# One load of k for three of four batches, pooled by GpSimd from its form with zeros

## The chip, the cores and the metric

The kernel runs on one core of a Trainium2 chip, as one program. The metric is its time on the device in microseconds (us), lower is better. A core has TensorE (matrix products, with a granted clock of 1.2 or 2.4 GHz), VectorE, ScalarE and GpSimd, each with a queue of instructions of its own that is worked off in order, and SyncE, which here issues the loads. In the profile's rows they are PE (PEld for its weight loads), DVE, ACT, POOL and SP.

## What is computed

An attention at two resolutions, then two expert layers. The change is in the attention, for 4 batches, 8 heads, 576 positions and 64 columns per head:

```python
q_d = q.reshape(B, H, Sd, factor, D).mean(axis=3)      # factor 4, Sd = 144; k_d, v_d alike
out_d = sm_attn(q_d, k_d, v_d)
out_up = np.repeat(out_d, factor, axis=2)
mask = np.abs(pos[:, None] - pos[None, :]) < factor
scores = np.where(mask, scale * np.matmul(q, k.transpose(0, 1, 3, 2)), -1000000000.0)
# softmax over the last axis, then
return (out_up + np.matmul(attn, v)).astype(np.float32)
```

So q, k and v are each needed twice: whole, for a local attention of 7 positions, and pooled over 4 neighbours, for the coarse one. Behind it the 2304 tokens are routed to 8 experts, and all go through a second layer.

## The kernel before

**Units.** Attention is a list of 60 units, made by `units`: a local unit `("l", b, i)` takes block `i` of 10 of batch `b`, all heads at once, and a pooled unit `("c", b, p)` takes head pair `p` of 4 (`p = 4` the rest of all pairs). The five pooled units of batch 0 come first; those of batch `b + 1` stand between the local units of batch `b`, behind its blocks 3, 5, 6, 8 and 9. Unit positions count through the list, so c1,0 (pooled, batch 1, pair 0) is four positions behind l0,0, c1,1 seven, c1,2 nine. `run` works it as a pipeline: scores (TensorE), softmax (VectorE takes the maximum, ScalarE the exponential with its sums), normalization (VectorE), transposes four positions later (TensorE, emptied by ScalarE), and the product with v six positions later (TensorE, added up by VectorE).

**Order.** Everything else hangs on a table `todo`: `at(i, f, ...)` calls `f` ahead of unit `i`. Each engine runs its instructions in the order in which they are written, so a position is an order, not a time. `i0` is the position of the batch's predecessor's first local unit; `KP`, `VP`, `V1` and the like are offsets to it, so that batch `b` is loaded and pooled while batch `b - 1`'s local units run.

**k in two forms.** A pooled unit multiplies with `ks`, a local one with `kb`. Both hold, for each head pair, two copies of 576 (or 144) columns, of which the first is zero in partitions 64 to 127 and the second in 0 to 63, so that one product gives both heads of a pair. There are two buffers of each. Before, k is loaded twice for batches 1 to 3: into `k` (128 partitions, one buffer; `load`), from which `prep` pools it into `ks`, and into the halves of `kb` that aren't zero (`load_kb`, twice 64 partitions). For batch 0 ScalarE copies it from `k` into `kb` (`copy_k`). The zeros are written once: of `ks` buffer 0 by VectorE, of `ks` buffer 1 and `kb` buffer 0 by GpSimd, of `kb` buffer 1 by DMAs from a zero tile (`zeros`).

GpSimd pools k in three instructions, an add of 288 elements over 128 partitions and two of 144 over 64:

```python
eng.tensor_add(t, src[:, :, 0:2], src[:, :, 2:4])
for r, o in dst:
    eng.tensor_add(o, t[r, :, 0], t[r, :, 1])
```

**v.** `load_vc` loads v for pooling into `vc`, which has one buffer, so the load for one batch waits until GpSimd (and for batch 0 VectorE too) has pooled the one before (`prep_v`, eight adds, into `vs`). `load_v` loads the local form. All loads are issued by SyncE, in order: one that waits holds those behind it.

Of the kernel before, what the change touches and what calls it, by code (L numbers as in the profile page):

```python
# [8 lines left out]
F32 = mybir.dt.float32  # L9
F32R = mybir.dt.float32r  # L10
BF = mybir.dt.bfloat16
# [8 lines left out]
B, H, S, D = 4, 8, 576, 64  # L20
NP = H // 2
DM = H * D
N = B * S
SC = S // 4
# [6 lines left out]
PN = ()  # L31
PC = ()
SQ = "VVVP"
SK = "PPPP"
KP = (3,5,7,9)
VP = (1,1,2,3,4,5,6,7)
V2, KD0 = 'VVVVPPPP', -1
V0, V1, ZP = 5, 4, 5
CPOS = (3,5,6,8,9)
SCB = 3  # L40
AVB = 2
# [13 lines left out]
class Attention:  # L55
# [4 lines left out]
    def __init__(self, tc, ctx, qT, kT, v, vc, c, xT):  # L60
        self.tc, self.nc, self.c, self.xT = tc, tc.nc, c, xT
        self.qT, self.kT, self.v, self.vc = qT, kT, v, vc
        nc = tc.nc
        self.ld = ctx.enter_context(tc.tile_pool(name="at_ld", bufs=1))
        self.wk = ctx.enter_context(tc.tile_pool(name="at_wk", bufs=1))
        self.ps = ctx.enter_context(tc.tile_pool(name="at_ps", bufs=1, space=PSUM))
        self.T = [dict() for _ in range(B)]
        self.kb = [self.ld.tile([128, NP, 2, S], F32, name=f"kb{i}") for i in range(2)]
        self.ks = [self.ld.tile([128, NP, 2, SC], F32, name=f"ks{i}") for i in range(2)]
        self.zero4 = self.ld.tile([128, S], F32, name="zero")  # L70
        nc.vector.memset(self.zero4, 0.0)
        self.zero = self.zero4.bitcast(BF)[:, :512]
        warm = self.wk.tile([1, 1], F32, name="warm")
        nc.vector.memset(warm, 0.0)
        nc.scalar.activation(warm, warm, AF.Exp)
# [12 lines left out]

    def zeros(self, t, eng):
        for h in range(2):  # L90
            z = t[64 * h:64 * h + 64, :, 1 - h]
            if eng is self.nc.sync:
                eng.dma_start(z, self.zero4[64 * h:64 * h + 64, None, :].to_broadcast(z.shape))
            else:
                eng.memset(z, 0.0)

    def copy_k(self, p):
        for h in range(2):
# [14 lines left out]
    def load(self, b):  # L113
        nc, ld, T = self.nc, self.ld, self.T[b]
        T["q"] = ld.tile([128, NP, S], F32, name="q", bufs=2)
        T["k"] = ld.tile([128, NP, S], F32, name="k", bufs=1)
        T["kb"], T["ks"] = self.kb[b % 2], self.ks[b % 2]
        T["v"] = ld.tile([128, NB, 4 * W], F32, name="v", bufs=2)
        T["qs"] = self.wk.tile([128, NP, SC], F32, name="qs", bufs=2)
        T["vs"] = self.wk.tile([HC, 2, DM], F32, name="vs", bufs=2)  # L120
        T["cT"] = self.wk.tile([128, NP, SC, 2], F32, name="cT", bufs=2)
        for p in range(NP):
            nc.sync.dma_start(T["q"][:, p], self.qT[NP * b + p])
            nc.sync.dma_start(T["k"][:, p], self.kT[NP * b + p])

    def load_kb(self, b):
        for h in range(2):
            r = slice(64 * h, 64 * h + 64)
            self.nc.sync.dma_start(self.T[b]["kb"][r, :, h], self.kT[NP * b:NP * b + NP, r].rearrange("p d s -> d p s"))

    def load_vc(self, b):
        t = self.T[b]["vc"] = self.ld.tile([HC, 2, 4, DM], F32, name="vc", bufs=1)
# [14 lines left out]

    def prep(self, b, p, x, eng):
        nc, T = self.nc, self.T[b]
        src = T[x][:, p].rearrange("p (s t) -> p s t", t=4)  # L150
        dst = [(slice(0, 128), T["qs"][:, p])] if x == "q" else [(slice(64 * h, 64 * h + 64),
                T["ks"][64 * h:64 * h + 64, p, h]) for h in range(2)]
        if eng.engine == nc.vector.engine:
            for r, o in dst:
                eng.tensor_reduce(o, src[r], AX.X, OP.add)
            return
        t = self.wk.tile([128, SC, 2], F32, name="half", bufs=2)
# [3 lines that stand above are left out]
# [123 lines left out]
    def run(self):  # L284
        nc = self.nc
        us = self.units()
        sts = [dict() for _ in us]
        n = len(us)
        pos = {u: i for i, u in enumerate(us)}
        todo = {}  # L290

        def at(i, f, *a):
            todo.setdefault(i, []).append(lambda: f(*a))

        V, P = nc.vector, nc.gpsimd
        self.load(0)
        self.load_vc(0)
        self.load_v(0)
        self.masks()
        self.zeros(self.ks[0], V)  # L300
        self.zeros(self.ks[1], P)
        for p in range(NP):
            at(p, self.prep, 0, p, "q", V)
            at(p, self.prep, 0, p, "k", V if p < 1 else P)
            at(p + 1, self.copy_k, p)
        at(3, self.zeros, self.kb[0], P)
        for x in range(8):
            at(V0 + x // 4, self.prep_v, 0, x, V if V2[x] == "V" else P)
        at(ZP, self.zeros, self.kb[1], nc.sync)
        for b in range(1, B):  # L310
            i0 = pos["l", b - 1, 0]
            at(i0 + KD0 if b == 1 else i0, self.load, b)
            at(i0 - 4 if b > 1 else i0 + KD0, self.load_vc, b)
            at(i0 + KD0 if b == 1 else i0, self.load_kb, b)
            at(i0 + KD0 if b == 1 else i0, self.load_v, b)
            for p in range(NP):
                at(i0 + KP[p], self.prep, b, p, "k", P if SK[p] == "P" else V)
                at(i0 + KP[p] + 1, self.prep, b, p, "q", P if SQ[p] == "P" else V)
            for x in range(8):
                at(i0 + VP[x] + (V1 if b == 1 else 0), self.prep_v, b, x, P)  # L320
        for i in range(n + LA + 1):
            for f in todo.get(i, ()):
                f()
            self.keep(HOT.get(i, 0))
            if i < n:
                self.scores(us[i], sts[i])
            if 0 <= i - LT < n:
                self.transposes(us[i - LT], sts[i - LT])
                self.evac(us[i - LT], sts[i - LT])
            if i < n and not NF:  # L330
                self.softmax(us[i], sts[i])
            if 0 <= i - LN < n:
                self.norm(us[i - LN], sts[i - LN])
            if i < n and NF:
                self.softmax(us[i], sts[i])
            if 0 <= i - LA < n:
                self.av(us[i - LA], sts[i - LA])
                self.combine(us[i - LA], sts[i - LA])
            self.done(i - LA)
        self.done(n)  # L340
# [838 lines left out]
```

## Time and profile before

| | |
|---|---|
| time, median of 3 runs | 899.79 us (895.54 to 900.38) |
| the profiled execution: its time, its span | 894.19 us, 892.5 us |
| TensorE, VectorE, ScalarE, GpSimd busy | 94%, 60%, 48%, 12% of the span |
| mean granted clock of TensorE | 0.973 of 2.4 GHz |
| DMA | 89.69 MB, mean 100 GB/s; 78.01 MB read from memory |
| loads of q, of k | 16 each of 288 KB |
| loads of kb, of vc | 6 of 576 KB, 4 of 1152 KB |
| zeros into kb | 2 of 576 KB |
| loads of v | 4 of 896 KB and 4 of 384 KB |

Attention takes about the first 150 us; routing and the experts follow. Shares over the whole span say little of it, so the rows below are cut by stretch. A busy TensorE is not one at its peak: at half the clock the same products keep it busy twice as long. In a chain of waits each piece is what the next one had to wait for.

### The profile page before, as it was taken

The numbers are of one execution on the slowest core, as the hardware profiler recorded it, in microseconds if no ns is written. First come the engines' busy times: TensorE is split into PE (matmuls) and PEld (weight loads), VectorE is DVE, ScalarE is ACT, GpSimd is POOL, SyncE is SP. The second block draws the span as 40 slices with busy tenths as digits, with TensorE's granted clock in tenths as the row PEclk, the third lists the DMA queues.
The fourth block names the chain that finished last, engine by engine and source line by source line (L and its number), as shares of the span: only waits on it lengthen the run. The fifth ranks groups of instructions, "written<-read, shape, count | busy, mean of one in ns | idle before, by whom it ended". The sixth has DMA issues, their size and how long they took to land.

```text
span 892.5 us, 16560 instructions
## 1 busy us (share of the span) xinstructions
PE 837.4 (94%) x6271; PEld 710.6 (80%) x6272; DVE 531.9 (60%) x1551; ACT 426.6 (48%) x1118; POOL 109.9 (12%) x175
## 2 busy tenths in 40 slices
PE   6899898789789999999999999999999999999996
PEld 2566566566568898988899988899888898899985
DVE  7887986667657986535565534865643742254222
ACT  4676786423445665434344344454344444454442
POOL 6445800011000011000110100200100110010001
PEclk9887999879999999999999999999999999999999
DMA  7998710747563353102041000740200520040000
GB/s 233 221 232 184 221 48 2 260 145 240 188 205 102 118 192 106 49 1 71 27 140 63 27 1 1 229 142 24 88 11 1 174 77 1 1 125 29 1 1 35
DMA packets 28415, 89.69 MB, mean 100 GB/s; under 512 B 3984, under 2 KB 3984, under 8 KB 28048
## 3 DMA queue, kind: packets, MB, share of 16 engines
q1 hardware_dynamic: 25360, 79.20, 29.7%
q0 software_dynamic: 2976, 9.44, 3.2%
q8 instruction: 49, 0.80, 0.4%
q14 instruction: 30, 0.25, 0.1%
HBM read 78.01 MB, written 9.44 MB: 98 GB/s over the span
## 4 chain that ended last, share of the span: by engine, by line
PE 77%; DVE 9%; DMA 7%; POOL 3%; ACT 3%; issue 1%; SPq 0%; POOLq 0%; ACTq 0%; DVEq 0%
PE h L843 33%; PE acc L856 31%; DMA raw<-in_wu_dram 3%; DMA vc<-in_vc_dram 3%; PE rt L558 2%; PE av L256 2%; PE sc L183 1%; PE pt L234 1%; POOL vc L146 1%; DVE p L225 1%; PE rt L742 1%; PE av L267 1%; PE rt L640 1%; PE sc L190 1%; DMA k<-in_kT_dram 1%
## 5 line engine op out<-in xcount | busy, mean ns | idle before, releaser
L880 DVE SCALAR_TENSOR_TENSOR g<-h,g 128x384 f32<-128x384 f32 x96 | 53.5, 557 | 174.3 <-ACT g L879 174.1
L878 ACT ACTIVATE g<-h,slope 128x384 f32<-128x384 f32 x96 | 55.9, 582 | 162.2 <-PE h L843 152.4
L843 PE MATMUL h<-yh,w2h 128*128 128x384 f32 x384 | 88.6, 352 | 0.0
L773 DVE TENSOR_TENSOR u<-raw,u 128x512 fp32r<-128x512 f32 x96 | 65.3, 688 | 37.4 <-ACT u L770 37.0
L856 PE MATMUL acc<-w2h,hh 128*128 128x512 f32 x288 | 84.9, 396 | 1.8 <-ACT hh L881 1.8
L856 PE MATMUL acc<-w2h,hl 128*128 128x512 f32 x288 | 84.8, 395 | 0.0
L856 PE MATMUL acc<-w2l,hh 128*128 128x512 f32 x288 | 84.7, 395 | 0.0
L843 PE MATMUL h<-yh,w2l 128*128 128x384 f32 x384 | 83.6, 339 | 0.0
L843 PE MATMUL h<-yl,w2h 128*128 128x384 f32 x384 | 83.5, 339 | 0.0
L883 DVE TENSOR_TENSOR hl<-g,hh 128x384 fp32r<-128x384 f32 x96 | 53.6, 558 | 48.4 <-ACT hh L881 48.4
L770 ACT ACTIVATE u<-raw 128x512 fp32r<-128x512 f32 x96 | 56.5, 624 | 47.9 <-PE acc L856 38.9
L881 ACT ACTIVATE hh<-g 128x384 fp32r<-128x384 f32 x96 | 50.3, 524 | 60.6 <-DVE g L880 60.6
L208 ACT ACTIVATE p<-sc,nm 128x64 f32<-128x64 f32 (+1 forms) x200 | 63.0, 330 | 31.7 <-DVE nm L206 28.6
L721 POOL DMA_INDIRECT xg<-xs,idx x24 | 23.5, 981 | 408.5 <-DVE idx L643 284.5
L843 PEld LDWEIGHTS h<-yh,w2h 128*128 128x128 f32 x384 | 66.4, 188 | 4.8 <-ACT yh L931 0.6
L843 PEld LDWEIGHTS h<-yl,w2h 128*128 128x128 f32 x384 | 69.1, 188 | 0.0
L843 PEld LDWEIGHTS h<-yh,w2l 128*128 128x128 f32 x384 | 69.0, 188 | 0.0
L856 PEld LDWEIGHTS acc<-w2h,hl 128*128 128x128 f32 x288 | 54.0, 187 | 13.4 <-DVE hl L883 0.3
L856 PEld LDWEIGHTS acc<-w2l,hh 128*128 128x128 f32 x288 | 54.0, 187 | 12.9
L856 PE MATMUL acc<-hh,u 128*128 128x288 f32 x384 | 61.2, 296 | 0.0
L879 ACT ACTIVATE g<-g,slope 128x384 f32<-128x384 f32 x96 | 59.2, 617 | 3.1
L856 PEld LDWEIGHTS acc<-w2h,hh 128*128 128x128 f32 x288 | 52.6, 187 | 7.7 <-ACT hh L881 3.2
(215 smaller groups left out, 1510.3 us busy)
## 6 DMA issues: line engine op xcount, KB each, us to landing
raw<-in_wu_dram SPq DMA_DIRECT2D x96, 512.0 KB, 4.2
q<-in_qT_dram SPq DMA_DIRECT2D x16, 288.0 KB, 6.4
k<-in_kT_dram SPq DMA_DIRECT2D x16, 288.0 KB, 4.8
vc<-in_vc_dram SPq DMA_DIRECT2D x4, 1152.0 KB
xs<-xrow SPq DMA_DIRECT2D x18, 256.0 KB, 2.3
v<-in_v_dram SPq DMA_DIRECT2D x4, 896.0 KB, 13.6
kb<-in_kT_dram SPq DMA_DIRECT2D x6, 576.0 KB, 16.0
v<-in_v_dram SPq DMA_DIRECT2D x4, 384.0 KB, 13.1
```

Of the source, the lines that this page charges most:

```text
L208: nc.scalar.activation(p[:, a], o[:, a], AF.Exp, bias=nm[:, a:a + 1], scale=st["scale"], accum_out=sm[:, a:a + 1])
L256: mm(o[r, p], T["v"][r, i, 64 * p:64 * p + 64], t[r, p // 2, w:w + n], start=True, stop=True)
L721: self.nc.gpsimd.indirect_dma_start(out=xg[g], out_offset=None, in_=self.r.xs, in_offset=bass.IndirectOffsetOnAxis(ap=idx[:, g:g + 1], axi ...
L770: self.nc.scalar.activation(hi, x, AF.Copy)
L773: self.nc.vector.tensor_sub(lo, x, hi.bitcast(F32))
L843: nc.tensor.matmul(p, w[a][:, 128 * kk:128 * kk + 128], v, start=(n == 0), stop=(n == len(order) - 1))
L856: self.nc.tensor.matmul(acc[d], x, y, start=(first and i == 0), stop=(last and i == len(terms) - 1))
L878: nc.scalar.activation(g, p, AF.Relu, scale=self.slope[:, 0, f:f + 1])
L879: nc.scalar.activation(g, g, AF.Copy, scale=self.slope[:, 1, f:f + 1])
L880: nc.vector.scalar_tensor_tensor(g, p, 0.0, g, op0=OP.max, op1=OP.add)
L881: nc.scalar.activation(hi, g, AF.Copy)
L883: nc.vector.tensor_sub(lo, g, hi.bitcast(F32))
```

## The change

Batches 1 to 3 load k once, into `kb`, in pieces of two head pairs, each ahead of the q of these pairs. GpSimd pools it from there, zeros included, so that the zeros of `ks` come out of the sum: an add of 576 elements over 128 partitions and one of 288. `load_kb` is gone, `k` is loaded for batch 0 alone, and the zeros of both `kb` buffers are written by GpSimd. The offsets change: `KP` by one position, `VP` and `V1` as shown, and of v's pooling the first half of the columns comes first.

```diff
-SK = "PPPP"
-KP = (3,5,7,9)
-VP = (1,1,2,3,4,5,6,7)
+KP = (2,4,6,8)
+VP = (1,3,4,5,7,8,9,10)
 V2, KD0 = 'VVVVPPPP', -1
-V0, V1, ZP = 5, 4, 5
+V0, V1 = 5, 2
...
     def zeros(self, t, eng):
         for h in range(2):
-            z = t[64 * h:64 * h + 64, :, 1 - h]
-            if eng is self.nc.sync:
-                eng.dma_start(z, self.zero4[64 * h:64 * h + 64, None, :].to_broadcast(z.shape))
-            else:
-                eng.memset(z, 0.0)
+            eng.memset(t[64 * h:64 * h + 64, :, 1 - h], 0.0)
...
-        T["k"] = ld.tile([128, NP, S], F32, name="k", bufs=1)
+        T["k"] = ld.tile([128, NP, S], F32, name="k", bufs=1) if b == 0 else None
...
         for p in range(NP):
+            if b > 0 and p % 2 == 0:
+                for h in range(2):
+                    r = slice(64 * h, 64 * h + 64)
+                    nc.sync.dma_start(T["kb"][r, p:p + 2, h],
+                                      self.kT[NP * b + p:NP * b + p + 2, r].rearrange("p d s -> d p s"))
             nc.sync.dma_start(T["q"][:, p], self.qT[NP * b + p])
-            nc.sync.dma_start(T["k"][:, p], self.kT[NP * b + p])
-
-    def load_kb(self, b):
-        for h in range(2):
-            r = slice(64 * h, 64 * h + 64)
-            self.nc.sync.dma_start(self.T[b]["kb"][r, :, h], self.kT[NP * b:NP * b + NP, r].rearrange("p d s -> d p s"))
+            if b == 0:
+                nc.sync.dma_start(T["k"][:, p], self.kT[p])
...
     def prep(self, b, p, x, eng):
         nc, T = self.nc, self.T[b]
+        if x == "k" and b > 0:
+
+            src = T["kb"][:, p].rearrange("p h (s t) -> p (h s) t", t=4)
+            t = self.wk.tile([128, 2 * SC, 2], F32, name="halves", bufs=1)
+            eng.tensor_add(t, src[:, :, 0:2], src[:, :, 2:4])
+            eng.tensor_add(T["ks"][:, p].rearrange("p h s -> p (h s)"), t[:, :, 0], t[:, :, 1])
+            return
...
         self.zeros(self.ks[0], V)
-        self.zeros(self.ks[1], P)
+        self.zeros(self.kb[0], P)
...
-        at(3, self.zeros, self.kb[0], P)
+        at(3, self.zeros, self.kb[1], P)
...
-        at(ZP, self.zeros, self.kb[1], nc.sync)
...
-            at(i0 + KD0 if b == 1 else i0, self.load_kb, b)
             at(i0 + KD0 if b == 1 else i0, self.load_v, b)
             for p in range(NP):
-                at(i0 + KP[p], self.prep, b, p, "k", P if SK[p] == "P" else V)
+                at(i0 + KP[p], self.prep, b, p, "k", P)
                 at(i0 + KP[p] + 1, self.prep, b, p, "q", P if SQ[p] == "P" else V)
-            for x in range(8):
-                at(i0 + VP[x] + (V1 if b == 1 else 0), self.prep_v, b, x, P)
+            for x, m in zip((0, 1, 4, 5, 2, 3, 6, 7), VP):
+                at(i0 + m + (V1 if b == 1 else 0), self.prep_v, b, x, P)
```

SyncE's queue for batch 1 and up to vc of batch 2, before (kb_95 is the buffer of the odd batches, kb_94 that of the even ones):

```order
L123 DMA q<-in_qT_dram 128x576
L124 DMA k<-in_kT_dram 128x576
...
L133 DMA vc<-in_vc_dram 72x4096
L129 DMA kb_95<-in_kT_dram 64x4x576 x2
L137 DMA v<-in_v_dram 128x768
L137 DMA v<-in_v_dram 128x1792
L93 DMA kb_95<-zero 64x4x576 x2
L133 DMA vc<-in_vc_dram 72x4096
```

and now:

```order
L120 DMA kb_95<-in_kT_dram 64x2x576 x2
L122 DMA q<-in_qT_dram 128x576 x2
L120 DMA kb_95<-in_kT_dram 64x2x576 x2
L122 DMA q<-in_qT_dram 128x576 x2
L128 DMA vc<-in_vc_dram 72x4096
L132 DMA v<-in_v_dram 128x768
L132 DMA v<-in_v_dram 128x1792
L128 DMA vc<-in_vc_dram 72x4096
```

Ahead of vc of batch 1 there are four loads of q and four into kb where there were four of q and four of k; the rest of kb and the zeros, which stood behind it, are gone.

GpSimd's queue from v of batch 0 to the fourth add on v of batch 1, before (ks_97 is the odd batches' buffer):

```order
L144 TENSOR_TENSOR vs<-vc 72x256
L158 TENSOR_TENSOR half<-k 128x288
L160 TENSOR_TENSOR ks_97<-half 64x144 x2
L158 TENSOR_TENSOR half<-k 128x288
L160 TENSOR_TENSOR ks_97<-half 64x144 x2
L146 TENSOR_TENSOR vc<-vc 72x2x256
L144 TENSOR_TENSOR vs<-vc 72x256
L146 TENSOR_TENSOR vc<-vc 72x2x256
L158 TENSOR_TENSOR half<-k 128x288
L160 TENSOR_TENSOR ks_97<-half 64x144 x2
L144 TENSOR_TENSOR vs<-vc 72x256
```

and now:

```order
L139 TENSOR_TENSOR vs<-vc 72x256
L149 TENSOR_TENSOR halves<-kb_95 128x576
L150 TENSOR_TENSOR ks_97<-halves 128x288
L141 TENSOR_TENSOR vc<-vc 72x2x256
L149 TENSOR_TENSOR halves<-kb_95 128x576
L150 TENSOR_TENSOR ks_97<-halves 128x288
L139 TENSOR_TENSOR vs<-vc 72x256
L149 TENSOR_TENSOR halves<-kb_95 128x576
L150 TENSOR_TENSOR ks_97<-halves 128x288
L141 TENSOR_TENSOR vc<-vc 72x2x256
L139 TENSOR_TENSOR vs<-vc 72x256
```

Of batch 1's four head pairs, the first two were pooled ahead of the first add on vc; now only the first is, and the second stands behind that add. In batches 2 and 3 the first add on vc stands ahead of all k in both kernels.

VectorE's queue where c1,0 is prepared, before (`mx` is a unit's maximum, `rc` and `p` the normalization of the unit before):

```order
L203 TENSOR_REDUCE mx<-sc 128x4
L206 TENSOR_SCALAR nm<-mx 128x4
L155 TENSOR_REDUCE qs<-q 128x144
L222 TENSOR_SCALAR rc<-sm 128x4
L223 RECIPROCAL rc<-rc 128x4
L225 TENSOR_TENSOR p<-p,rc 128x256
L203 TENSOR_REDUCE mx<-sc 128x2
```

and now:

```order
L208 TENSOR_SCALAR nm<-mx 128x4
L157 TENSOR_REDUCE qs<-q 128x144
L224 TENSOR_SCALAR rc<-sm 128x4
L225 RECIPROCAL rc<-rc 128x4
L227 TENSOR_TENSOR p<-p,rc 128x256
L205 TENSOR_REDUCE mx<-sc 128x4
L208 TENSOR_SCALAR nm<-mx 128x4
L224 TENSOR_SCALAR rc<-sm 128x4
L225 RECIPROCAL rc<-rc 128x4
L227 TENSOR_TENSOR p<-p,rc 128x256
L205 TENSOR_REDUCE mx<-sc 128x2
```

The pooling of q for c1,0 stands one local unit further ahead of the maximum of c1,0, the last row of both.

## Rows read from the trace of the kernel before

**Rows 1.** Busy time by stretch: us, busy us of each engine, granted clock, DMA share, GB/s.

```profile
32.30:35.70 3.40, 3.40 (x21) 2.03 (x20) 1.66 (x6) 2.93 (x16) 0.00 (x0) 0.50 0.98 162
...
45.90:52.70 6.80, 6.36 (x48) 3.80 (x48) 6.53 (x15) 3.34 (x20) 5.81 (x9) 0.50 0.92 191
...
69.80:80.00 10.20, 10.20 (x100) 7.36 (x102) 7.74 (x19) 4.97 (x26) 9.40 (x15) 0.50 1.03 189
...
105.00:150.00 45.00, 44.90 (x712) 32.41 (x712) 36.04 (x134) 36.64 (x190) 5.32 (x24) 1.00 0.16 55
```

**Rows 2.** What VectorE waited for, 22 to 106 us: total, times, longest.

```profile
DVE xT L278 <- PE av L256: 2.9, 6, 1.0
DVE mx L203 <- PE sc L183: 2.8, 4, 1.4
DVE mx L203 <- PE sc L190: 1.8, 3, 1.1
```

**Rows 3.** TensorE in order of time: start us, us, line, shapes, count, idle before.

```profile
32.05 1.08 PE L190 MATMUL sc<-ks,qs 128*128 128x288 f32 x2 [1.23 <-DVE rc L222]
...
39.06 0.75 PE L190 MATMUL sc<-ks,qs 128*128 128x288 f32 x2
...
44.34 0.75 PE L190 MATMUL sc<-ks,qs 128*128 128x288 f32 x2 [1.73 <-POOL ks L160]
...
65.42 1.08 PE L363 MATMUL tk<-xT,g 128*32 128x128 f32 x32
68.82 0.75 PE L190 MATMUL sc<-ks,qs 128*128 128x288 f32 x2 [2.32 <-POOL ks L160]
```

**Rows 4.** The chain of waits, 20 to 70 us: start us, us, what.

```profile
25.32 13.69 DMA vc<-in_vc_dram
...
52.11 11.29 DMA vc<-in_vc_dram
```

**Rows 5.** Busy time by stretch again, for the DMA columns at the end.

```profile
0.00:22.00 22.00, 13.62 (x62) 5.95 (x63) 15.90 (x32) 10.68 (x28) 14.46 (x28) 1.00 0.79 235
...
68.00:76.00 8.00, 7.18 (x74) 5.42 (x74) 5.81 (x14) 4.00 (x22) 7.51 (x12) 0.61 1.05 170
84.00:90.00 6.00, 6.00 (x78) 4.17 (x78) 5.28 (x22) 5.45 (x30) 0.00 (x0) 1.00 0.48 113
92.00:98.00 6.00, 5.64 (x77) 3.81 (x75) 5.79 (x12) 3.99 (x24) 5.63 (x8) 1.00 1.00 335
```

**Rows 6.** GpSimd's groups: shapes, count, busy us, mean ns, idle before.

```profile
L146 POOL TENSOR_TENSOR vc<-vc 72x512 f32<-72x512 f32 x14 | 18.9, 1350 | 33.4 <-DMA vc<-in_vc_dram 33.4
...
L160 POOL TENSOR_TENSOR ks<-half 64x144 f32<-64x144 f32 x30 | 13.6, 453 | 2.1
L158 POOL TENSOR_TENSOR half<-k 128x288 f32<-128x288 f32 x15 | 10.5, 699 | 6.1 <-DMA k<-in_kT_dram 5.8
L144 POOL TENSOR_TENSOR vs<-vc 72x256 f32<-72x256 f32 x14 | 10.4, 743 | 1.1
L95 POOL MEMSET kb<- 64x2304 f32 x2 | 4.0, 2012 | 0.1
```

**Rows 7.** VectorE in order of time, the maximum of c1,1.

```profile
41.48 0.45 DVE L203 TENSOR_REDUCE mx<-sc 128x2 f32<-128x288 f32 x1
```

**Rows 8.** VectorE's groups, 90.4 to 107 us, while GpSimd pools.

```profile
L225 DVE TENSOR_TENSOR p<-p,rc 128x256 f32<-128x256 f32 (+1 forms) x7 | 4.5, 645 | 0.2
L206 DVE TENSOR_SCALAR nm<-mx 128x4 f32<-128x4 f32 (+1 forms) x7 | 3.7, 527 | 0.2
L222 DVE TENSOR_SCALAR rc<-sm 128x4 f32<-128x4 f32 (+1 forms) x7 | 3.3, 478 | 0.0
```

**Rows 9.** The same groups, 112 to 146 us, GpSimd idle.

```profile
L225 DVE TENSOR_TENSOR p<-p,rc 128x256 f32<-128x256 f32 (+1 forms) x18 | 7.8, 432 | 0.6
L206 DVE TENSOR_SCALAR nm<-mx 128x4 f32<-128x4 f32 (+1 forms) x18 | 3.0, 169 | 0.6
L222 DVE TENSOR_SCALAR rc<-sm 128x4 f32<-128x4 f32 (+1 forms) x19 | 3.0, 159 | 0.0
```

More of the change, by code (lines that the diff above doesn't have):

```diff
@@ L69, in __init__ @@
         self.ks = [self.ld.tile([128, NP, 2, SC], F32, name=f"ks{i}") for i in range(2)]
-        self.zero4 = self.ld.tile([128, S], F32, name="zero")
-        nc.vector.memset(self.zero4, 0.0)
-        self.zero = self.zero4.bitcast(BF)[:, :512]
+        self.zero = self.ld.tile([128, 512], BF, name="zero")
+        nc.vector.memset(self.zero, 0.0)
         warm = self.wk.tile([1, 1], F32, name="warm")
```

## The prediction

> **What bounds the kernel now.** I read the clock and busy times by stretch first, then who waited for whom on VectorE and TensorE, then the chain of waits, and last the groups of GpSimd. Times are those of the profiled execution, 892.5 us long. Units of attention are written l1,0 (local, batch 1, block 0) and c2,0 (pooled, batch 2, head pair 0).
>
> From 105 us to the end of attention at 150 TensorE is busy 44.9 of 45 us at the full clock, and the DMA engines hardly work [rows 1]. The change touches no instruction there, nor behind it, where routing and the experts run: that part can only start earlier or later. What can be won lies ahead of 105 us.
>
> There the DMA engines are full (share 0.92 to 1.03 in three stretches), the granted clock is at its lower level, 1.2 GHz, in 32.3 to 35.7, 45.9 to 52.7 and 69.8 to 80.0 us, and VectorE is busy 6.53 of 6.8 us in the middle one [rows 1]. A full DMA system is no proof that loads bound anything. The better question is when VectorE, whose work per unit stays as it is, stood still. Between 22 and 106 us it waited for TensorE 2.9 + 2.8 + 1.8 = 7.5 us [rows 2]. **That is the most that earlier data can give**: all the rest of those 84 us it worked, or stood locked (below). Of it, 1.7 us lie in 32.3 to 35.7 us, 0.3 in 45.9 to 52.7, and 2.5 in 69.8 to 80.0 [rows 1].
>
> TensorE's stops in front of that: c1,0 at 32.05 waited 1.23 us for VectorE, c1,2 at 44.34 waited 1.73 us and c2,0 at 68.82 waited 2.32 us, both for GpSimd's pooled k [rows 3]. The clock was at 1.2 GHz within 1.6 us of each stop's end. The chain of waits says why GpSimd was late: vc has one buffer, so its load starts when GpSimd has pooled the batch before, takes 13.69 us the first time and 11.29 us the second, and GpSimd's queue stands behind it [rows 4].
>
> **The change, part by part.**
>
> *Bytes.* Three k loads of 1.18 MB and the 1.18 MB of zeros go. The kind of load matters: in a stretch with little but loads into 64 partitions (kb) 170 GB/s moved at a share of 1.05, in one with q and k into 128 partitions mostly 335 at 1.00 [rows 5]. So the change drops the cheap form: a batch saves 1.18 / 0.335 = 3.5 us of DMA time and keeps kb's 1.18 / 0.170 = 6.9. None of this is on the path by itself; it counts through three landings.
>
> *vc of batch 1.* It is issued when vc of batch 0 is used up, 25.3 us in both kernels [rows 4]. Ahead of it now stand kb and q of batch 1, issued early since k's single buffer no longer holds SP. Batch 0's 4.85 MB take 4.85 / 0.235 = 20.6 us at the rate of the first 22 us [rows 5], so the queue ahead of vc empties at 20.6 + 6.9 + 3.5 = 31.0. For vc itself the ends are 1.18 / 0.335 = 3.5 us and 1.18 / 0.113 = 10.4 us, the rate where vc was left alone at the end of a load [rows 5]. I take 7, between them: landing at 38.0 us, ends 34.5 and 41.4, against 39.0 in the trace. The removed megabytes do not bring it forward, as zeros and kb stood behind it before.
>
> *k of head pair 1 now stands behind vc on GpSimd* (the order above). The new first add has 576 elements; 288 took 699 ns and 144 took 453, which gives 699 + 246 x 2 = 1190 ns by that line and, by vc's 1350 ns for 512, 1.5 us as the other end. I take 1.19, as it has the same strides. With a second add of 0.70 a head pair is pooled in 1.9 us, against 699 + 2 x 453 = 1.6 [rows 6]. So c1,1 can start at 38.0 + 1.35 + 1.9 = 41.2 instead of 39.06 [rows 3]. VectorE took that unit's maximum only at 41.48 [rows 7]; now it can at 41.2 + 0.7 = 41.9. **Term: +0.4 us**, ends -2.5 (landing at 34.5, the idle time before 40 us won too) and +3.9 (at 41.4).
>
> *q pooled one unit earlier on VectorE.* This ends the 1.23 us at c1,0, and could win the 1.7 us of idle time behind it. But the next step stops at c1,1 anyway, so I cost it at nothing; it is in the -2.5 above. What is late next is that landing of vc.
>
> *vc of batch 2 and c2,0.* GpSimd's work from the landing of vc on is 4 x (1.35 + 0.74) + 3 x 1.9 + 1.2 for q (0.70 + 0.45, as for k) = 15.3 us, so the next vc is issued at 53.3 (52.1 before [rows 4]), into a queue that is now empty: 7 us, 60.3. kb's first half follows when l0,9 has read its buffer, and needs 0.59 / 0.170 = 3.5 us: 63.8. k of pair 0 is pooled by 65.7. TensorE is there at 65.42 + 1.08 = 66.5 in the trace [rows 3], at 66.9 with the term above. The wait of 2.32 us goes: c2,0 starts 1.9 us earlier than at 68.82. **Term: -1.9 us from the trace's place** (the +0.4 included). If TensorE does not stop, nothing in the trace's pattern sends the clock down at 69.8, and the 2.5 us that VectorE idled there go as well: **-2.5**. Ends: 0 and -2.5.
>
> *Locks.* While GpSimd computes without a break, three of VectorE's instructions per unit are longer: 645, 527 and 478 ns [rows 8] instead of 432, 169 and 159 [rows 9]. Over seven each that is 7 x (213 + 358 + 319) = 6.2 us in 16.6, or 0.38 us per us of GpSimd. The change adds 12 x 0.3 = 3.6 us of pooling: **+1.4**, ends 0 and +3.6. The memsets (2.0 us each [rows 6]): kb0's move ahead of the first k, where GpSimd waited for the load; kb1's take their old place; ks1's go. Nothing.
>
> The Trainium skill (SBUF — State Buffer, section "SBUF: two separate sides") speaks against the change here: VectorE and GpSimd share a port pair as an exclusive lock, and the loser stands for the whole instruction. By that rule a longer GpSimd instruction may cost VectorE its full length, so this term would be up to +3.6 instead of +1.4, and the sum -0.8 instead of -3.0.
>
> *The last pooling.* vc of batch 3 comes earlier, but kb waits for l1,9 and then needs its 3.5 us before k of pair 0; by the same steps GpSimd ends about 2 us later than in the trace, where TensorE alone is the bound [rows 1]; 2 x 0.38 lies within the locks' ends. Nothing.
>
> **Sum:** -1.9 - 2.5 + 1.4 = -3.0 us. Against the profiled execution's own 894.2 us that is 891.2. The median of the three runs is 899.8, 5.6 above it, and measured runs are compared with that: 899.8 - 3.0 = **896.8 us**.
>
> **Rivals.**
> - *The clock stays up everywhere.* vc lands near 34.5, c1,0 and c1,1 do not stop, and most of the 7.5 us is won, with the same locks: -7.5 + 1.4 = -6.1 us, 893.7. For it: all three stretches at 1.2 GHz follow a stop that the change touches. Against: VectorE idled 0.3 us in the second of them, so a faster TensorE wins nothing there. 0.27.
> - *The first vc stops TensorE* (the side against). The landing of vc of batch 1 decides: from 41.48 - 0.7 - 1.9 - 1.35 = 37.5 us on, c1,1 is later for VectorE than in the trace. At 41.4 the term is +3.9 and TensorE stands 44.6 - 39.1 = 5.5 us; the clock falls, and VectorE idles 2.5 us more, as in 69.8 to 80.0 [rows 1]. The lateness swallows the 2.3 us at c2,0, and the locks add their 1.4: 3.9 + 2.5 - 2.3 + 1.4 = +5.5, or 905.3. For it: GpSimd's order puts k of pair 1 behind vc, where the trace had it in front. Against: vc must be as slow as where it was alone. 0.14.
> - *VectorE pays for all of GpSimd's time.* Each added us meets a VectorE instruction that stands for it: -1.9 - 2.5 + 3.6 = -0.8, 899.0. For it, three kinds of instruction grow by up to 358 ns where GpSimd computes [rows 8, 9]; against, the sum of it was 0.38 us per us and not 1. So 0.12. (The page of the Trainium skill named above would have this as the worst case.)
> - *The change does not do what it says.* GpSimd then would read k from somewhere else; the order shows it reads kb. Below 0.01, and left out.
>
> **How the numbers follow.** My forecast has 0.47, its neighbours as above. 0.5% is 4.5 us, about what a measurement of this kernel can tell from no change. Forecast and third rival lie within it (0.59, less 0.02 for runs that scatter by 2 us: 0.57), the first rival is faster (0.27, plus 0.02: 0.29), the second slower (0.14). The range must hold the runs' own scatter, 895.5 to 900.4 in the three shown: it reaches from 890.5, somewhat below the first rival, to 902, which leaves out the second rival's far half.
>
> **What would show it.** Right: no wait of TensorE for GpSimd at c2,0, no stretch at 1.2 GHz near 70 us, batch 2's first local unit some 3 us earlier, and from there the same distances to the end. The wait for vc on GpSimd shorter at the second and third batch, and about as long at the first. VectorE's three instructions still long wherever GpSimd computes. Wrong: a wait of TensorE at c1,1 over 3 us for the pooled k, or attention ending within 1 us of where it did; and, for the faster side, no stretch at 1.2 GHz before 105 us at all.

## The result, and the profile after

The changed kernel takes 904.5 us (median of 20 runs) where the kernel before, run beside it, takes 899.8 (20 runs): **ratio 1.0075, 95% interval 1.0051 to 1.0099, so slower by 0.75%**. Run again on another chip it had 1.0079 (1.0052 to 1.0105). The ratio is worked out from the runs in the faster of the chip's two states alone, so it isn't the quotient of the two medians, which is 1.0052. Forecast was 896.8 us within 890.5 to 902; it came out slower and above that range.

The profiled execution has a span of 903.3 us (892.5 before) at a mean granted clock of 0.960 of 2.4 GHz (0.973), and moves 84.97 MB (89.69). To see where the 10.8 us lie, both spans are cut at the same pieces of work: VectorE's maximum of l0,0, of c1,1, of c2,0, of l3,0, and 25.5 us behind the last, where attention ends. Busy time by stretch of the kernel before (us, busy us of TensorE, its weight loads, VectorE, ScalarE and GpSimd, granted clock, DMA share, GB/s):

```profile
0.00:26.20 26.20, 17.61 (x85) 8.22 (x87) 19.99 (x37) 11.71 (x32) 18.20 (x33) 0.93 0.82 244
26.20:41.50 15.30, 13.58 (x157) 9.11 (x155) 11.77 (x40) 11.95 (x64) 3.87 (x6) 0.89 1.03 213
41.50:69.60 28.10, 23.61 (x287) 15.72 (x286) 24.58 (x71) 18.90 (x96) 15.76 (x22) 0.88 0.98 217
69.60:125.60 56.00, 52.90 (x691) 36.87 (x689) 49.80 (x154) 40.40 (x205) 28.50 (x57) 0.91 0.65 172
125.60:151.10 25.50, 25.19 (x437) 18.38 (x436) 18.39 (x71) 19.30 (x101) 0.00 (x0) 1.00 0.01 3
```

and of the changed kernel:

```profile
0.00:29.00 29.00, 20.07 (x94) 8.70 (x95) 17.69 (x37) 11.82 (x32) 19.39 (x29) 0.88 0.90 212
29.00:50.60 21.60, 16.55 (x120) 11.14 (x120) 12.98 (x40) 11.85 (x63) 6.43 (x7) 0.50 0.68 168
50.60:80.50 29.90, 25.82 (x330) 17.54 (x328) 24.97 (x69) 18.96 (x96) 17.01 (x20) 0.90 0.59 123
80.50:137.60 57.10, 54.20 (x671) 37.70 (x671) 51.90 (x154) 40.20 (x207) 29.28 (x49) 0.85 0.44 127
137.60:163.10 25.50, 25.24 (x437) 18.42 (x436) 18.41 (x71) 19.29 (x101) 0.00 (x0) 1.00 0.01 3
```

The last stretch is alike, as forecast, and what lies behind it is 1.2 us shorter in the changed kernel's profile. Ahead of it the change loses 2.8, 6.3, 1.8 and 1.1 us. In a second profile of the changed kernel (j2_changed_again, below) the four losses are 0.3, 6.4, 5.6 and 1.0 us: that of the second stretch comes again, those of the first and third are not the same from one execution to the next. VectorE does the same 37, 40, 69 or 71, and 154 instructions in each, and from the second stretch on it is busy longer with them: by 1.2, 0.4 and 2.1 us.

The second stretch has TensorE at 1.2 GHz throughout, and this chain of waits of the changed kernel (start us, us, what), which answers to [rows 4]:

```profile
29.60 16.17 DMA vc<-in_vc_dram
...
45.90 1.26 POOL vc L141
47.16 1.29 POOL halves L149
...
48.53 0.67 POOL ks L150
...
49.24 1.33 PE sc L192 x2
```

vc of batch 1 takes 16.17 us against 13.69, and k of pair 1 is pooled behind it. TensorE's stops in order of time (the last brackets: idle us and who ended them):

```profile
49.24 1.33 PE L192 MATMUL sc<-ks,qs 128*128 128x288 f32 x2 [4.77 <-POOL ks L150]
...
76.89 0.75 PE L192 MATMUL sc<-ks,qs 128*128 128x288 f32 x2
...
80.94 0.48 PE L376 MATMUL tk<-ident,lT 128*128 128x128 f32 x1 [2.47 <-ACT lT L367]
```

c1,1 waits 4.77 us for its k; c2,0, at 76.89, waits for nothing, where it waited 2.32 us [rows 3]. And TensorE stops all the same four us later, for ScalarE: the rows by stretch show what follows. (Two products of one shape take 1.33 us for c1,1, at 1.2 GHz, and 0.75 for c2,0, at 2.4: 1.8 times as long at half the clock, not quite twice.)

```profile
80.30:90.50 10.20, 9.56 (x88) 6.82 (x90) 9.31 (x21) 5.46 (x30) 9.50 (x12) 0.50 0.36 127
```

GpSimd's groups, answering to [rows 6]:

```profile
L141 POOL TENSOR_TENSOR vc<-vc 72x512 f32<-72x512 f32 x14 | 19.4, 1382 | 37.0 <-DMA vc<-in_vc_dram 37.0
L149 POOL TENSOR_TENSOR halves<-kb 128x576 f32<-128x576 f32 x12 | 13.9, 1158 | 8.1 <-DMA kb<-in_kT_dram 8.1
L139 POOL TENSOR_TENSOR vs<-vc 72x256 f32<-72x256 f32 x14 | 10.4, 743 | 0.7
L150 POOL TENSOR_TENSOR ks<-halves 128x288 f32<-128x288 f32 x12 | 8.3, 694 | 0.9
```

The new add takes 1.16 us (1.19 was estimated), a pair 1.85. Now VectorE and GpSimd side by side, in order of time, in the changed kernel:

```profile
53.01 0.72 POOL L139 TENSOR_TENSOR vs<-vc 72x256 f32<-72x256 f32 x1
...
53.20 1.91 DVE L227 TENSOR_TENSOR p<-p,rc 128x256 f32<-128x256 f32 x1
...
53.69 1.14 POOL L149 TENSOR_TENSOR halves<-kb 128x576 f32<-128x576 f32 x1
...
54.91 0.73 POOL L150 TENSOR_TENSOR ks<-halves 128x288 f32<-128x288 f32 x1
```

A normalization that takes 0.43 us with GpSimd idle [rows 9] takes 1.91 and ends at 55.11, 0.28 us behind the end of the add of 576 elements. So there are two suspects: **loads** (kb in 64 partitions ahead of q and vc, hence a late vc and the stop at c1,1) and **long adds** (what VectorE stands for behind them).

### The profile page after: what moved, and what is told of

It is laid out like the page before. It is cut to its first block, busy times and chain, and to the rows that moved or that the text cites. A ratio compares the mean times of both kernels' runs of the same rounds, so it can differ in the third digit from the quotient of the medians.

```text
span 903.3 us, 16556 instructions
## 1 busy us (share of the span) xinstructions
PE 845.8 (94%) x6271; PEld 715.6 (79%) x6272; DVE 533.5 (59%) x1551; ACT 426.9 (47%) x1118; POOL 115.6 (13%) x163
## 2 busy tenths in 40 slices
DMA packets 26239, 84.97 MB, mean 94 GB/s; under 512 B 3856, under 2 KB 3856, under 8 KB 25872
## 4 chain that ended last, share of the span: by engine, by line
PE 76%; DMA 10%; DVE 7%; ACT 3%; issue 1%; POOL 1%; SPq 0%; ACTq 0%; POOLq 0%
PE h L843 32%; PE acc L856 31%; DMA raw<-in_wu_dram 4%; DMA kb<-in_kT_dram 2%; PE rt L558 2%; PE av L258 2%; DMA vc<-in_vc_dram 2%; PE sc L185 2%; PE pt L236 2%; DVE p L227 1%; DMA q<-in_qT_dram 1%; PE av L269 1%; PE rt L742 1%; DMA xs<-xrow 1%; PE sc L192 1%
## 5 line engine op out<-in xcount | busy, mean ns | idle before, releaser
L938 POOL DMA_INDIRECT out_dram<-o,ib x18 | 18.4, 1024 | 326.4 <-DVE o L936 323.8
```

What stands on the lines that cost most here:

```text
L938: st = nc.gpsimd.indirect_dma_start(out=self.out, out_offset=bass.IndirectOffsetOnAxis(ap=self.ib[:, t:t + 1], axis=0), in_=o, in_offset=None)
```

## The experiments

Ratios are to runs of the kernel before on the same chip, with their 95% interval. A single execution scatters by several us: the profiled one of the kernel before took 894.2 us where its median is 899.8. So ratios decide, and profiles say where to look.

**First set: are the loads issued too early, and does k belong ahead of v?** In the changed kernel nothing holds SyncE at batch 1's loads. e1_hold makes kb's second buffer be written late (one element, by GpSimd, which loads then wait for); e2_order pools v of batch 1 two positions later, so that k of pair 1 stands ahead of it again; e3_both does both.

e1_hold, in the changed kernel behind the zeros of kb's second buffer:

```diff
+        at(3, P.memset, self.kb[1][0:1, 0:1, 0, 0:1], 0.0)
```

e2_order, in the changed kernel:

```diff
-V0, V1 = 5, 2
+V0, V1 = 5, 4
```

> Changed kernel, but SyncE can issue batch 1's loads only after GpSimd has zeroed the kb buffer (near 19 us instead of 8.8). Theory: the early loads of batch 1 slow vc of batch 0, which in the changed kernel came 4 us later than before. Then GpSimd's first add on vc starts near 19 to 20 us again (23.3 in the changed kernel), the next vc is issued near 25.3 to 26 (29.6), TensorE's wait for pooled k at c1,1 falls from 4.8 us to 1 to 3, and the ratio to the kernel before falls from 1.0075 to about 1.001 to 1.004. Rival, the order on GpSimd alone: the wait at c1,1 stays over 4 us and the ratio at 1.006 to 1.009.

> Changed kernel, but in batch 1 all adds on vc stand two units later, so that the second head pair's k is pooled ahead of the first of them. Theory (early loads): GpSimd's first add on vc of batch 0 still starts near 23.3 us and TensorE still waits over 2 us for VectorE's pooled v, but the wait at c1,1 goes: ratio 1.002 to 1.005. Rival, the order on GpSimd alone: all of the loss goes, ratio 0.995 to 1.000.

> Both edits, the held loads and the later adds on vc. Theory: neither of the two stops is left, batch 1's first local unit comes near 57 to 59 us (68.4 in the changed kernel, 58.0 before), ratio 0.995 to 1.000. If locks by GpSimd's longer adds were what costs: ratio above 1.003 still.

Measured: e1_hold 1.0071 (1.0042 to 1.0100), e2_order 1.0035 (1.0000 to 1.0070), e3_both 1.0049 (1.0022 to 1.0076). Holding the loads wins nothing: in e1_hold's profile GpSimd's first add on vc of batch 0 starts at 19.2 us, as expected, and c1,1 stops for 3.5 us, but the time stays. Nor does that add start late in every execution of the changed kernel: at 23.3 us in the first profile, at 20.5 in that of j2_changed_again. In e2_order c1,1 doesn't stop:

```profile
39.31 1.33 PE L192 MATMUL sc<-ks,qs 128*128 128x288 f32 x2
```

and about half of the loss seems to go, though its interval and that of the change overlap. The rest stays without that stop, and e3_both stands above the 1.003 that it was to exceed if GpSimd's longer adds were what costs.

**Second set: the order of loads, in the kernel before.** e4_kb_first issues batch 1's kb ahead of its q and k; e5_q_first its q ahead of its k (e6_q_first5 is the same kernel, timed). g3_q_ahead puts each pair of q ahead of its kb, in e2_order.

e4_kb_first:

```diff
...
+            if b == 1:
+                at(i0 + KD0, self.load_kb, b)
...
-            at(i0 + KD0 if b == 1 else i0, self.load_kb, b)
+            if b > 1:
+                at(i0, self.load_kb, b)
```

e5_q_first and e6_q_first5:

```diff
-            nc.sync.dma_start(T["k"][:, p], self.kT[NP * b + p])
+            if b != 1:
+                nc.sync.dma_start(T["k"][:, p], self.kT[NP * b + p])
+        if b == 1:
+            for p in range(NP):
+                nc.sync.dma_start(T["k"][:, p], self.kT[NP * b + p])
```

g3_q_ahead, in e2_order:

```diff
-            if b > 0 and p % 2 == 0:
+            nc.sync.dma_start(T["q"][:, p], self.qT[NP * b + p])
+            if b > 0 and p % 2 == 1:
...
-                    nc.sync.dma_start(T["kb"][r, p:p + 2, h],
-                                      self.kT[NP * b + p:NP * b + p + 2, r].rearrange("p d s -> d p s"))
-            nc.sync.dma_start(T["q"][:, p], self.qT[NP * b + p])
+                    nc.sync.dma_start(T["kb"][r, p - 1:p + 1, h],
+                                      self.kT[NP * b + p - 1:NP * b + p + 1, r].rearrange("p d s -> d p s"))
```

> Kernel before, but batch 1's two kb loads (64 partitions each, 1.18 MB together) are issued ahead of its q and k, so early, near 9 us. Theory that loads into half the partitions slow what is ahead of them: GpSimd's first add on vc of batch 0 starts 2 to 5 us later than 19.1 us. Theory that a queue serves in order: it stays within 0.5 us.

> Kernel before, but batch 1's four q loads (128 partitions, 1.18 MB together) are issued ahead of its k, so early, near 9 to 12 us. Theory of the half partitions: the first add on vc of batch 0 moves by less than 1 us from 19.1. Rival, any early bytes slow vc: it starts 2 to 5 us later, as with kb first.

> Kernel before with batch 1's four q loads ahead of its four k loads (the one look gave 890.95 us beside 900.08), now timed. If the early q helps: 0.993 to 0.998. If the one look was scatter: 0.998 to 1.002.

> The changed kernel with the later adds on vc in batch 1 (as in the run before with that edit, 1.0035), and in every batch each pair of q loads ahead of the pair's two kb loads. Theory: VectorE's wait for q at c2,0 (1.3 to 6.3 us in the changed kernel and its variants) goes, but the pooled k comes later instead, so c2,0 moves by less than 2 us: ratio 1.001 to 1.005. If q behind kb was the rest of the loss: 0.997 to 1.001.

Measured: e4_kb_first one run, 904.9 against 900.1; e5_q_first one run, 891.0 against 900.1, which in twelve runs (e6_q_first5) became 1.0001 (0.9970 to 1.0032). One run can't tell 1% here, so e4_kb_first is inconclusive in time. In its profile GpSimd's first add on vc of batch 0 starts at 20.1 us against 19.1 in the kernel before, which neither of its two theories had; in e5_q_first's it starts at 19.9, within the 1 us of the theory of the half partitions. g3_q_ahead had 1.0044 (1.0019 to 1.0069): the order of q and kb isn't the rest of e2_order's loss.

**Third set: the parts alone.** g2_zeros is the kernel before with GpSimd writing all zeros; g1_k_twice is that plus the change's positions for k and v, with k still loaded twice and pooled from `k`.

g2_zeros, in the kernel before:

```diff
+        self.zeros(self.kb[0], P)
...
-        at(3, self.zeros, self.kb[0], P)
+        at(3, self.zeros, self.kb[1], P)
...
-        at(ZP, self.zeros, self.kb[1], nc.sync)
```

g1_k_twice, beyond that:

```diff
-KP = (3,5,7,9)
-VP = (1,1,2,3,4,5,6,7)
+KP = (2,4,6,8)
+VP = (1,3,4,5,7,8,9,10)
...
-V0, V1, ZP = 5, 4, 5
+V0, V1, ZP = 5, 2, 5
...
-            for x in range(8):
-                at(i0 + VP[x] + (V1 if b == 1 else 0), self.prep_v, b, x, P)
+            for x, m in zip((0, 1, 4, 5, 2, 3, 6, 7), VP):
+                at(i0 + m + (V1 if b == 1 else 0), self.prep_v, b, x, P)
```

> The kernel before with the change's zeros alone: both kb buffers and ks zeroed by GpSimd, no DMA of zeros (1.18 MB less for the DMA engines, one memset pair more ahead of GpSimd's first k). Zeros harmless: 0.996 to 1.001. If GpSimd's memsets cost: 1.003 and up, by GpSimd's first k later than 9 us.

> The changed kernel with its main part undone: batches 1 to 3 load k a second time into 128 partitions and are pooled from there, in three GpSimd instructions per head pair; zeros by GpSimd, offsets and order of the pooling of v stay as changed. Theory 1 (pooling k from kb is what costs, since a head pair now waits for slower loads and its adds are longer): ratio 0.995 to 1.001 against the kernel before. Theory 2 (GpSimd's order alone, k of pair 1 behind the first add on vc): the loss stays, 1.004 to 1.009, with TensorE's wait of 3 to 5 us at c1,1.

Measured: g2_zeros 0.9979 (0.9947 to 1.0010), g1_k_twice 0.9977 (0.9942 to 1.0011). Zeros and positions cost nothing that these intervals show; the whole loss, 1.0075 / 0.9977 or about 1.0%, comes with loading k once and pooling it from kb.

**Fourth set: long adds or loads.** Both start from g1_k_twice. h1_long_adds makes only the adds on k as long as the changed kernel's (it leaves out the zeros in the other half of ks); h3_k_halves changes only the form of k's loads.

h1_long_adds:

```diff
+        if x == "k" and b > 0:
+            src = T["k"][:, p].rearrange("p (s t) -> p s t", t=4)[:, None].to_broadcast([128, 2, SC, 4])
+            t = self.wk.tile([128, 2, SC, 2], F32, name="halves", bufs=1)
+            eng.tensor_add(t, src[:, :, :, 0:2], src[:, :, :, 2:4])
+            eng.tensor_add(T["ks"][:, p], t[:, :, :, 0], t[:, :, :, 1])
+            return
```

h3_k_halves:

```diff
+            if b > 0 and p % 2 == 0:
+                for h in range(2):
+                    r = slice(64 * h, 64 * h + 64)
+                    nc.sync.dma_start(T["k"][r, p:p + 2],
+                                      self.kT[NP * b + p:NP * b + p + 2, r].rearrange("p d s -> d p s"))
...
-            nc.sync.dma_start(T["k"][:, p], self.kT[NP * b + p])
+            if b == 0:
+                nc.sync.dma_start(T["k"][:, p], self.kT[p])
```

> The kernel of g1_k_twice (k loaded twice, pooled from its own buffer k), in which GpSimd's adds on k of batches 1 to 3 are made as long as the changed kernel's: 576 and 288 elements over 128 partitions, source still k, read twice. It leaves out the zeros in the other half of ks in these batches, so the pooled attention isn't the reference's; the number and shapes of all products stay. Theory 'longer adds' (GpSimd's time, its locks on VectorE and the later ks are what the change costs): ratio to the kernel before 1.004 to 1.010, against 0.998 for g1_k_twice, and a unit c1,1 or c1,2 that waits for the pooled k. Rival 'slow landing' (loads into 64 partitions stand ahead of q and vc, and what hangs on them comes late): ratio 0.996 to 1.001, since its loads are those of g1_k_twice.

> The kernel of g1_k_twice with one thing changed: k of batches 1 to 3 is loaded into its buffer k in the form in which the changed kernel loads kb (64 partitions at a time, two head pairs in a load, ahead of the q of these pairs). The adds stay short, and kb is loaded as before. Theory 'slow landing': ratio to the kernel before 1.003 to 1.008, vc of batch 1 added later than 42 us or k of pair 1 waited for by GpSimd. Rival 'longer adds': ratio 0.997 to 1.002, since the adds are those of g1_k_twice.

Measured: **h1_long_adds 1.0051 (1.0023 to 1.0080), h3_k_halves 0.9999 (0.9970 to 1.0029)**. The first interval lies wholly above g1_k_twice's (they ran on two chips, each against its own runs of the kernel before): the length of the adds alone costs 0.74%, three quarters of the loss, with the loads untouched. Taken together, the two intervals leave room for anything from 0.3 to 1.2% (an estimate). Longer adds also make the pooled k later, and c1,1 stops in h1_long_adds too:

```profile
41.76 1.33 PE L196 MATMUL sc<-ks,qs 128*128 128x288 f32 x2 [4.29 <-POOL ks L154]
```

But against g1_k_twice this stop makes nothing late: the maximum of c1,1 comes 16.4 us behind that of l0,0, in g1_k_twice 17.7. h3_k_halves isn't told apart from g1_k_twice, though in its profile c1,1 stops for 10.53 us:

```profile
48.13 1.33 PE L196 MATMUL sc<-ks,qs 128*128 128x288 f32 x2 [10.53 <-POOL ks L166]
```

A long stop of TensorE that early, then, isn't a loss of that size. A smaller cost of the form of the loads isn't excluded: between g1_k_twice and h3_k_halves, on two chips, the intervals leave room for up to some 0.7% (an estimate).

How the adds cost it is in VectorE's busy time for the same work, maximum of l0,0 to maximum of l3,0, 262 or 263 instructions in each kernel (columns as above: VectorE's is the third, GpSimd's the fifth). The kernel before:

```profile
26.20:125.60 99.40, 90.09 (x1132) 61.70 (x1129) 86.14 (x263) 71.25 (x365) 48.13 (x83) 0.90 0.80 191
```

changed:

```profile
29.00:137.60 108.60, 96.57 (x1119) 66.37 (x1119) 89.85 (x262) 71.01 (x365) 52.73 (x74) 0.80 0.53 134
```

g1_k_twice:

```profile
24.90:120.60 95.70, 88.34 (x1121) 61.05 (x1121) 84.02 (x263) 69.68 (x365) 50.23 (x86) 0.89 0.73 187
```

h1_long_adds:

```profile
26.70:131.90 105.20, 92.66 (x1125) 63.17 (x1121) 91.05 (x262) 70.51 (x365) 51.14 (x72) 0.85 0.66 164
```

From g1_k_twice to h1_long_adds GpSimd is busy 0.9 us longer, and VectorE 7.0. That is no rate per us of GpSimd. Of the 9.5 us by which the stretch is longer, these 7.0 are VectorE's busy time and 2.5 its idle time. The instruction that grows most is the normalization, from 554 ns in g1_k_twice

```profile
L225 DVE TENSOR_TENSOR p<-p,rc 128x256 f32<-128x256 f32 (+1 forms) x46 | 25.5, 554 | 1.6
```

to 633 in h1_long_adds:

```profile
L231 DVE TENSOR_TENSOR p<-p,rc 128x256 f32<-128x256 f32 (+1 forms) x46 | 29.1, 633 | 1.6
```

For a table by GpSimd's instruction, each VectorE instruction between 22 and 135 us is taken at its time above that of its like when undisturbed (the fastest tenth of its shape), and the excess put down to the GpSimd instruction that it overlaps (shared out by the overlap, where there are several):

| GpSimd's add | kernel | mean us | VectorE's excess per add, us |
|---|---|---|---|
| k, 64x144 | before, g1_k_twice | 0.46, 0.45 | 0.07, 0.05 |
| k (and q), 128x288, first add | before, g1_k_twice | 0.70, 0.75 | 0.16, 0.18 |
| k, 128x288, second add | changed, h1_long_adds | 0.69, 0.70 | 0.16, 0.20 |
| k, 128x576 | changed, h1_long_adds | 1.16, 1.21 | 0.59, 0.59 |
| v, 72x256 | before, g1_k_twice | 0.74, 0.74 | 0.21, 0.19 |
| v, 72x512 | before, g1_k_twice, changed | 1.32, 1.31, 1.38 | 0.75, 0.75, 0.54 |

An add 1.65 times as long (1.16 against 0.70) costs VectorE 3.7 times as much. A head pair costs it 0.16 + 2 x 0.07 = 0.30 us in the kernel before and 0.59 + 0.16 = 0.75 in the changed one: 12 x 0.45 = 5.4 us for 12 pairs. The first add on vc gives some of that back in the changed kernel (12 x 0.21 = 2.5 us).

**Fifth set: length against time.** If it is length, then cutting an add in two must help although GpSimd then needs longer in all; if VectorE pays per us of GpSimd, it must hurt. i1_split cuts both adds on k in the changed kernel, i2_split_order in e2_order, i3_v_split cuts the first add on vc in g1_k_twice, and j1_all_split has both cuts, in e2_order. j2_changed_again is the changed kernel beside the latter.

The adds on k:

```diff
-            eng.tensor_add(t, src[:, :, 0:2], src[:, :, 2:4])
-            eng.tensor_add(T["ks"][:, p].rearrange("p h s -> p (h s)"), t[:, :, 0], t[:, :, 1])
+            for h in range(2):
+                c = slice(SC * h, SC * h + SC)
+                eng.tensor_add(t[:, c], src[:, c, 0:2], src[:, c, 2:4])
+                eng.tensor_add(T["ks"][:, p, h], t[:, c, 0], t[:, c, 1])
```

The first add on vc:

```diff
-            eng.tensor_add(vc[:, j, 0:2, d], vc[:, j, 0:2, d], vc[:, j, 2:4, d])
+            for m in range(2):
+                eng.tensor_add(vc[:, j, m, d], vc[:, j, m, d], vc[:, j, m + 2, d])
```

> The changed kernel with each of its two adds on k cut in two, one per half of ks: 288, 144, 288, 144 elements over 128 partitions in place of 576 and 288; loads, order and results as changed. GpSimd's time for a head pair grows from 1.85 us to about 2.3. Theory 'length' (VectorE stands longer behind one long GpSimd add than behind two short ones): by the lengthening of VectorE's instructions in the traces, 0.16 to 0.18 us per add of 288 and 0.05 to 0.07 per add of 144 against 0.59 and 0.16 per add of 576 and 288, a pair costs VectorE 0.47 us and not 0.75; 12 pairs make -3.4 us, ratio to the kernel before 1.002 to 1.005 where the changed kernel has 1.0075. Rival 'time' (every us of GpSimd costs VectorE the same): 12 x 0.45 x 0.38 = +2.0 us, ratio 1.008 to 1.011.

> The same cut made in the kernel of e2_order (the changed kernel with batch 1's pooling of v two positions later, 1.0035). Theory 'length': ratio 0.998 to 1.001, about the time of the kernel before. Rival 'time': 1.004 to 1.007.

> The kernel of g1_k_twice (0.9977), in which the other long instruction of GpSimd, the first add on vc (512 elements over 72 partitions, 1.33 us, behind which VectorE's instructions are longer by 0.75 us), is cut into two of 256 (0.74 us each, 0.19 to 0.24 us of lengthening). Theory 'length': 13 x (0.75 - 2 x 0.23) = -3.8 us, ratio 0.992 to 0.995. Rival 'time': GpSimd needs 13 x 0.15 = 2 us more, +0.7 us, ratio 0.997 to 1.000.

> The kernel of i2_split_order (1.0024) with the first add on vc cut in two as well, as in i3_v_split: no add of GpSimd on k or v of batches 1 to 3 has over 288 elements. Theory 'length': VectorE gains about 13 x (0.41 - 0.20) = 2.7 us more by the lengthening in the traces of i2_split_order and i3_v_split; ratio to the kernel before 0.997 to 1.001. Rival 'time': GpSimd needs 2 us more, ratio 1.003 to 1.006.

> The changed kernel itself, on the same chip and beside the same runs of the kernel before as j1_all_split. If the ratios of runs on different chips can be compared, 1.005 to 1.010; and its ratio less that of j1_all_split is what length and order of GpSimd's adds together cost the change: by 'length' 0.006 to 0.010, by 'time' 0.001 to 0.004.

Measured: i1_split 1.0048 (1.0017 to 1.0079), i2_split_order 1.0024 (0.9991 to 1.0058), **i3_v_split 0.9950 (0.9919 to 0.9982)**, and on one chip **j1_all_split 1.0016 (0.9985 to 1.0048) against j2_changed_again 1.0079 (1.0052 to 1.0105)**. Each of the first three lies below its parent, none by more than its interval; by "time" all were to lie above. The last two are apart: cuts and order together bring back 0.63%, near the lower end of what "length" gave. i1_split and i3_v_split stand at the slow end of its bands, i2_split_order and j1_all_split 0.14% and 0.06% beyond them. The order alone had 0.40% in e2_order, so of the 0.63% the cuts' own share isn't told from nothing by these intervals. So the sign is that of length, and the size is less than the table's. The stretch from l0,0 to l3,0 shows VectorE's part, in i1_split

```profile
29.00:135.60 106.60, 94.50 (x1121) 65.13 (x1121) 83.16 (x263) 70.51 (x365) 57.65 (x98) 0.80 0.53 134
```

and in j1_all_split:

```profile
26.20:126.40 100.20, 89.92 (x1129) 61.66 (x1128) 80.34 (x262) 70.63 (x364) 58.69 (x108) 0.88 0.54 143
```

GpSimd is busy 4.9 and 6.0 us longer than in the changed kernel, VectorE 6.7 and 9.5 shorter. The same cut in e2_order, whose row is

```profile
24.70:134.70 110.00, 97.92 (x1119) 67.42 (x1119) 93.72 (x262) 71.05 (x365) 52.67 (x74) 0.80 0.52 135
```

against that of i2_split_order:

```profile
28.30:131.60 103.30, 94.00 (x1121) 64.58 (x1121) 81.74 (x262) 70.62 (x364) 58.23 (x98) 0.83 0.55 142
```

makes GpSimd busy 5.6 us longer and VectorE 12.0 shorter. So in these profiles VectorE's busy time follows the length of the adds and not their sum. The time doesn't follow to the same extent: the ratios fall by 0.27% in i1_split (2.4 us) and 0.11% in i2_split_order (1.0 us). A part of what the cuts free VectorE stands idle (stretch less busy time): 13.3 us in the kernel before, 18.8 in the changed one, 23.4 in i1_split, 19.9 in j1_all_split, where VectorE is busy 5.8 us less than in the kernel before and the ratio is still 1.0016. Among these waits are, in i1_split's profile, TensorE's stop at c1,1 (6.6 us) and a wait of VectorE for q (3.8 us).

i3_v_split is faster than the kernel before, and the only one here whose interval says so. It keeps k loaded twice. That the cut makes it faster than g1_k_twice isn't shown: the intervals overlap, and the quotients of the medians, 0.9940 and 0.9938, don't differ.

## Why the prediction was wrong

- **"Locks": wrong, and the main error.** The step took one rate, 0.38 us of VectorE per us of GpSimd, from a stretch with adds of several lengths, times the 12 x 0.3 = 3.6 us that pooling grows, and got +1.4. The 0.3 us are a difference of sums; what counts is that an add of 0.70 us and two of 0.45 gave way to one of 1.16 and one of 0.69. By the table that is +5.4 us, by h1_long_adds against g1_k_twice 0.74% or 6.7 us, by VectorE's busy time in the changed kernel's profile 3.7 us against the kernel before and 5.8 against g1_k_twice. The far end, +3.6, was too low as well: it bounded the cost by the added time, while VectorE pays anew for each longer add. The Trainium skill (SBUF — State Buffer, "SBUF: two separate sides") has the shared port pair held for a whole instruction; the normalization at 53.20, which ended only behind the long add, agrees, as far as one instruction goes. Read rightly that rule speaks of the length of an instruction, where the text used it as a bound on the sum.
- **The rows were there.** [Rows 6] had the add of 1350 ns and the ones of 453, and the excess could have been split by them. The first add on vc alone made 9.0 of some 17 us. (A second reading was too short: the 7.5 us of [rows 2] aren't all of VectorE's idle time. It was busy 72.33 of the 84 us, so 11.7 were idle; no term of the sum changes by that.)
- **vc of batch 1, +0.4: too low.** Landing was put 12.7 us behind the issue (38.0 - 25.3), with 16.1 (41.4 - 25.3) as the far end. It took 16.17 in the changed kernel's profile and 16.92 in that of j2_changed_again, beyond that end; it was also issued later, by 4.3 and 1.3 us. c1,1's maximum came 21.6 us behind that of l0,0, against 15.3. What of it stays at the end isn't settled: e2_order takes the stop away and stands at 1.0035, but h3_k_halves stops twice as long and stands at 0.9999.
- **c2,0's wait goes, -1.9: the wait went, the time didn't.** TensorE stops 4 us later, for lT of the router's unit, and the clock is at 1.2 GHz for 80.3 to 90.5 us. From c1,1 to c2,0 the changed kernel lost time (29.9 us against 28.1) where 1.9 were to be won. So **"the clock does not fall at 69.8", -2.5, was wrong**: what is late next was taken to be nothing.
- **Right:** the zeros and the positions at nothing (g2_zeros, g1_k_twice); nothing won by 4.7 MB less; behind l3,0 the same distances, to 1.2 us. **Right in part:** VectorE as the engine that decides ahead of 105 us. In h1_long_adds its busy time and the loss grow alike (7.0 and 6.7 us), but the cuts free more of it than they win.
- **The rival "the first vc stops TensorE"** gave 905.3, and its sign of recognition, c1,1 over 3 us late for the pooled k, was seen. But its sum has the locks at 1.4 and the stop at 6.4, and h1_long_adds, whose loads are untouched, shows three quarters of the loss. Its number was near by luck: its reasons were largely not those that the runs show. "VectorE pays for all of GpSimd's time" named the right place, with too small a price.

Open: with every long add cut, the changed kernel stands at 1.0016 and i3_v_split, which loads k twice, at 0.9950. These 0.7% lie between kernels on different chips and hold the form of k's loads, the order of the adds, the late vc and the wait for q; no run parts them. Nor do the runs show which part of the idle time that the cut kernels have more of hangs on which load.

## What to carry to other kernels

Where VectorE is the bound and GpSimd computes beside it, price each GpSimd instruction by its own length, not by GpSimd's total: here two adds of 0.70 us cost VectorE 0.3 us and one of 1.16 us cost 0.6. Cutting a long GpSimd instruction in two is cheap to try, and VectorE's busy time fell with it each time (by 6.7 and 12.0 us in the changed kernel and in e2_order); that the kernel's time falls as well was too small to show here for any cut alone. Work taken off the loads and put on the engine that holds up VectorE was a loss here, though it saved 4.7 MB: ask of an engine off the critical path whom it holds up.

## What was not expected of the hardware

- VectorE's excess grows faster than the length of GpSimd's add: 0.05 to 0.07 us at 0.45, 0.16 to 0.20 at 0.70, 0.59 at 1.16 to 1.21. That GpSimd's lock is the cause is argued from the side-by-side rows; that length counts is shown in time by h1_long_adds, and by the cuts in VectorE's busy time alone.
- One normalization stood for 1.91 us against 0.43, through the rest of one GpSimd add and the whole of the next.
- vc of batch 1 took 15.6, 16.2 and 16.9 us from its issue in three profiles with loads into 64 partitions ahead of it (e1_hold, changed, j2_changed_again), and 13.7 behind q and k in 128 [rows 4].
- One execution of one kernel was 1% faster than the kernel before and its twelve runs were not (e5_q_first, e6_q_first5).
